# Chunk 0's layer norm: rows centred first, then transposed by products with diagonal matrices of 1/std

## The chip, the cores and the metric

The kernel runs on one NeuronCore of a Trainium2 chip. A core has five engines with queues of their own: TensorE (PE; its weight loads are shown apart as PEld), VectorE (DVE), ScalarE (ACT), GpSimd (POOL) and SyncE (SP, which here issues the transfers). The metric is the device time of one execution in microseconds; lower is better.

## What is computed

The input x has 2048 rows of 512 bf16 values. A first layer norm is followed by a spectral filter (a real two-dimensional Fourier transform, a product with complex weights, and the inverse transform), added to x. The sum h goes through a second layer norm and a two-layer network with a squared ReLU, added to h:

```python
x = A_x
h = x + irfft2(rfft2(_layernorm(x)) * (A_w_r + 1j * A_w_i))
u = _layernorm(h)                      # (h - m) / sqrt(v + 1e-5), over 512 columns
r = relu(einsum("bsd,df->bsf", u, B_w1) + B_b1)      # 512 -> 1792
out = h + einsum("bsf,fd->bsd", r * r, B_w2) + B_b2  # 1792 -> 512
```

The layer norms have no weights of their own.

## The kernel before

The 2048 rows are 16 groups g of 128 rows. The transforms are products with cosine and sine tables that are made on the chip. After the inverse transform along the rows lies its intermediate result T2 in SBUF; from there on everything is done group by group, and the groups are taken together in five chunks for the network: (0,1), (2,3,4), (5..8), (9..12), (13..15) (`CHUNKS`, L696). Two matrix products with W1 and W2 per chunk make up most of the remaining work.

The stretch between the last transform step and the first product with W1 is called the drain here. In it chunk 0 is on its own way:

- `d5` (L709, tasks pd-g-e): two products for each of the two column parities e of group g, into a PSUM bank. `deo` (L716, tasks EO-g-e) copies each result, 128x256, to SBUF.
- `d6` (L799, tasks py-g-0, py-g-1, py-g-2): four products that add up in one bank (tag `sg`, two banks, one for each group): x itself through the identity matrix (k=0), the even columns (k=1), the odd columns (k=2, two products). The bank py-g then holds h for group g.
- Statistics. The mean of h is known beforehand (nm1 is its negative). For group 0 ScalarE squares h minus the mean with a sum as a second output (task ss-0, L814, profile line L674); for group 1 VectorE uses the batch-norm statistics (tasks st2 and ss-1, L817 and L819). ScalarE takes the root (sd-0-g, L820), VectorE the reciprocal (r2-0-g, L823) and the product nr2 = nm1 * rs2 (L825).
- `un0` (L828): the normalised rows u, 128x512 bf16; ScalarE for group 0 (L833), VectorE for group 1 (L831).
- `tr0` (L839): four 128x128 transposes of each group on TensorE, into a bank of tag `po` (two banks), with bf16 results.
- `et0` (L846): one copy of 128x512 for each group to UT, the operand of the first products with W1. ScalarE or VectorE, whichever the planner finds ready.
- `hb` (L836): h + b2, from the bank py-g, on VectorE, after UT is complete. With its end the `sg` bank is free.

The first two blocks f of the product with W1 (`up`, L904) are split by group for chunk 0: the half of group 0 is task pf-f, the half of group 1 is task ph-0-f. pf-0 writes a bank of tag `ph`, pf-1 one of tag `po`; later blocks use `ph` and the two `sg` banks in turn.

Chunk 1's groups 2, 3 and 4 already begin in the drain: four products (`s5`, L736, tasks p5-g, tag `pp` with three banks), a copy of half of them on ScalarE (`od`, L745), two sums on VectorE (`lv1`, L750, tasks q-g-0 and q-g-1), and nine small products (`s6`, L759, tasks p6-g) into another `pp` bank.

The order of the instructions is set by a planner, `Plan` (L34 to L137). Each task has an engine (or a choice of two), a cost, what it reads, and a priority. `run` (L89) takes, again and again, over all engines, the task with the earliest planned start `r`; if two engines have the same start, VectorE goes first (L118). A result that passes from one engine to another costs `HOP` (L39: PE 0.20, ACT 0.17, DVE 0.15), on the same engine 0.1 for VectorE and ScalarE. The tasks are emitted in the order in which they are picked, and `pin` (L22) keeps each engine in that order. The planner knows how many banks a tag has and gives the one that comes free first (`slot`, L77). The framework adds the waits between engines.

`bank` (L687) hands out the PSUM banks. If the planner expects TensorE to stand idle for over 0.4 us before the task, it puts products of a zero matrix into the new bank first (L689, L690), one for each 0.0625 us of 0.6 of the gap, at most 20. They are called fillers below.

Of the kernel before, what the change touches and what calls it, by code (L numbers as in the profile page):

```python
# [9 lines left out]
ALU = mybir.AluOpType  # L10
ACT = mybir.ActivationFunctionType
# [22 lines left out]
class Plan:  # L34
# [13 lines left out]
    def add(self, eng, w, fn, reads=(), writes=(), prio=0.0, alloc=None, at=0.0, shared=False, lag=0.0,  # L48
            uses=(), order=()):
        many = isinstance(eng, tuple)  # L50
        ways = dict(zip(eng, w)) if many else {eng: w}
        t = dict(many=many, eng=None, ways=ways, w=0.0, fn=fn, reads=list(reads), writes=list(writes), prio=prio, alloc=alloc, at=at,
                 shared=shared, lag=lag, end=None, order=list(order), n=len(self.tasks))
        self.tasks.append(t)
        for k in t["writes"]:
            self.made.setdefault(k, []).append(t)
        for k in set(t["reads"]) | set(t["writes"]) | set(uses):
            self.use.setdefault(k, []).append(t)
# [29 lines left out]

    def run(self):  # L89
        left = {}  # L90
# [6 lines left out]
        while any(left.values()):  # L97
            best = None
            for e, ts in left.items():
                cand = []  # L100
                for t in ts:
                    r = self.ready(t, e)
                    if r is None:
                        continue
                    if t["alloc"]:
                        s, _ = self.slot(t["alloc"][0])
                        if s is None:
                            continue
                        r = max(r, s)
                    r = max(r, self.free[e])  # L110
                    cand.append((r, t))
                    if r <= self.free[e] + 1e-9:
                        break
# [11 lines left out]
            if t["alloc"]:  # L125
                tag, key = t["alloc"]
                _, old = self.slot(tag)
                if old is not None:
                    self.held[tag].remove(old)
                self.held[tag].append(key)  # L130
            self.gap = r - self.free[e]
            t["end"] = r + t["w"]
            self.free[e] = t["end"]
            for k in t["ways"]:
                left[k].remove(t)
            self.log.append((r, t["end"], e, t["writes"]))
            t["fn"](*([e] if t["many"] else []))  # L137
# [3 lines left out]
def kernel(  # L141
# [47 lines left out]
    st2 = persist.tile([P, 6], FP32, name="st2")  # L189
    EO = persist.tile([P, 2, 2, 256], BF16, name="EO")  # L190
    junk = persist.tile([P, D], BF16, name="junk")
    fz = persist.tile([P, 512], BF16, name="fz")
# [295 lines left out]
    for pr, first in ((0, 1), (1, 1), *((p, 0) for p in range(8))):  # L488
# [45 lines left out]
        if pr == 0 and first:  # L534
# [11 lines left out]
            for u in range(2):  # L546
# [3 lines left out]
                    order=[("X", 0, 0)] * u, writes=[("X", 0), ("Xu", u)] + [("X", 0, 0)] * (1 - u),  # L550
                    alloc=None if u else ("AB", ("X", 0)))
        elif pr > 0 and not first:
# [29 lines left out]
            def ea(pr=pr, ab=ab):  # L582
                t = buf(fwd, ab, "AB", [P, 2, 2, 256], BF16, 3)
                sc.copy(t[:].rearrange("p u r c -> p (u r c)"), T["p3", pr][:])  # L584
            act(0.93, ea, z + 1, reads=[("p3", pr)], writes=[ab], alloc=("AB", ab))
            if ab[0] == "AB":
# [6 lines left out]
                for h in range(2):  # L593
                    dve(0.34, lambda pr=pr, h=h: bf(pr, h), z, reads=[("AB", pr)],
                        order=[("Xh", pr)] * h,
                        writes=[("X", pr)] + [("Xh", pr)] * (1 - h), alloc=("X", ("X", pr)) if h == 0 else None)

# [8 lines left out]
        for u in range(2) if pr == 0 else ():  # L606
            dve(0.61, lambda u=u, prod=prod: prod(0, u, 1), z, reads=[("Xu", u), ("Wn", 0), ("Wn", 1)], uses=[("X", 0)],
                order=["mh"] * u, writes=[("m", 0)] + ["mh"] * (1 - u), alloc=None if u else ("m", ("m", 0)))
        if pr:
# [6 lines left out]
        for r in range(2):  # L616
            dve(0.34, lambda pr=pr, r=r: zz(pr, r), z, reads=[("m", pr)],
                order=[("Zh", pr)] * r,
                writes=[("Z", pr)] + [("Zh", pr)] * (1 - r), alloc=("Z", ("Z", pr)) if r == 0 else None)
        if pr > 0:  # L620
# [8 lines left out]
            for h in range(2):  # L629
                dve(0.34, lambda pr=pr, h=h: fold(pr, h), z, reads=[("Z", pr)],  # L630
                        order=[("Mh", pr)] * h,
                    writes=[("M", pr)] + [("Mh", pr)] * (1 - h), alloc=("M", ("M", pr)) if h == 0 else None)

# [29 lines left out]
        if pr < 7:  # L663
            act(0.97, et, z + 3, reads=[("p4", pr)], writes=["T2", "T2a"])
        else:
            for h in range(2):
                eng = ("ACT", "DVE")[h]
                add(eng, (0.24, 0.22)[h], lambda et=et, h=h, eng=eng: et(COPY[eng], 7, 0, 2, 2 * h, 2 * h + 2), prio=z,
                    reads=[("p4", 7, h)], writes=["T2a"])
                add(eng, (0.52, 0.6)[h], lambda et=et, h=h, eng=eng: et(COPY[eng], 7, 2, G, 2 * h, 2 * h + 2), prio=z + 90,  # L670
                    reads=[("p4", 7, h)], order=["T2a"], writes=["T2"])

# [56 lines left out]
    for c, (a, b) in enumerate(CHUNKS):  # L729
# [3 lines left out]
        for g in range(a, b):  # L733
            z = late + g
            if c > 0:
# [18 lines left out]
                for i in range(2):  # L754
                    dve(0.36, lambda g=g, i=i: lv1(g, i), z, reads=[("p5", g), ("od", g)],
                        order=[("qh", g)] * i + [("un", 1)] * (c == 1),
                        writes=[("q", g), ("qh", g)] if i == 0 else [("q", g)], alloc=("qb" if g in BY_PE2 else "q", ("q", g)) if i == 0 else None)

# [15 lines left out]
                else:  # L774
# [11 lines left out]
                    for k in range(4):  # L786
                        dve(0.25, lambda g=g, k=k: lv2(g, k), z, reads=[("q", g)], order=[("Rh", g)], writes=[("R", g)])

# [8 lines left out]
        if c == 0:  # L797
            for g in range(2):
# [9 lines left out]
                for k in range(3):  # L808
                    add("PE", 0.22, lambda g=g, k=k, d6=d6: d6(g, k),
                        reads=[["ident"], [("EO", g, 1), ("EI", 3)], [("EO", g, 0)]][k],  # L810
                        order=[("pd", 1, 0) if k == 0 else ("pd", g, 0)] + [("py", g, j) for j in range(k)], uses=[("py", g)],
                        writes=[("py", g, k)], prio=-5000.0 + g - 50 * (k == 0), alloc=("sg", ("py", g)) if k == 0 else None)
                if g == 0:
                    act(0.9, lambda: sq_of(T["py", 0][:], 0), -30.0, reads=[("py", 0, 2), "nm1", "sqrt"], writes=[("ss", 0)],  # L814
                        uses=[("py", 0)])
                else:
# [7 lines left out]
                    writes=[("r2", 0, g)])  # L824
                dve(0.16, lambda g=g: ve.tensor_tensor(nr2[:, g:g + 1], nm1[:, g:g + 1], rs2[:, g:g + 1], ALU.mult), -30.0,  # L825
                    reads=[("r2", 0, g), "nm1"], writes=[("n2", 0, g)])

                def un0(g=g):  # L828
                    u = buf(ffn, ("u", 0), "u2", [P, 4, D], BF16, 2) if g == 0 else T["u", 0]
                    if g:  # L830
                        ve.tensor_scalar(u[:, 1, :], T["py", 1][:], nm1[:, 1:2], rs2[:, 1:2], ALU.add, ALU.mult)  # L831
                    else:
                        sc.activation(u[:, 0, :], T["py", 0][:], ACT.Identity, scale=rs2[:, 0:1], bias=nr2[:, 0:1])  # L833
                add(("ACT", "DVE")[g], (0.6, 0.7)[g], un0, reads=[("r2", 0, g), ("n2", 0, g)], writes=[("un", g)] + ["una0"] * (1 - g),
                    order=["una0"] * g, uses=[("py", g), ("u", 0)], prio=-30.0, alloc=None if g else ("u2", ("u", 0)))
                dve(0.69, lambda g=g: ve.tensor_tensor(hb[:, g, :], T["py", g][:], b2b[:], ALU.add), -10.0,  # L836
                    reads=[("un", g), ("FW", 3)], order=[("UT", 0)] * OWN, writes=[("hb", g)], uses=[("py", g)])

                def tr0(g=g):  # L839
                    p = bank(("pt", 0, g), "po", 2, BF16)  # L840
                    for d in range(ND):
                        pe.transpose(p[:, P * d:P * d + P], T["u", 0][:, g, bass.ts(d, P)], ident[:])
                add("PE", 0.24, tr0, reads=[("un", g)], writes=[("pt", 0, g)], uses=[("u", 0)], prio=early + 3,
                    alloc=("po", ("pt", 0, g)))

                def et0(e, g=g):  # L846
                    u = buf(ffn, ("UT", 0), "UT", [P, 4, ND, P], BF16, 2) if g == 0 else T["UT", 0]
                    COPY[e](flat(u[:, g]), T["pt", 0, g][:, 0:D])
                add(("ACT", "DVE"), (0.57, 0.43), et0, reads=[("pt", 0, g)], order=["UT0a"] * g,
                    writes=[("UT", 0), "UT0b" if g else "UT0a"], prio=-30.0, alloc=None if g else ("UT", ("UT", 0)))  # L850
        else:
# [8 lines left out]
            for g in range(a, b):  # L860
                def un(e, g=g, a=a, c=c):
# [8 lines left out]
                    order=[("una", a)] * (g > a), uses=[("u", c)],  # L870
                    writes=[("un", g)] + [("una", a)] * (g == a), prio=z, shared=True, alloc=("u2", ("u", c)) if g == a else None)
            for g in range(a, b):
# [3 lines left out]
                def turn(c=c, i=g - a):  # L876
                    u = buf(ffn, ("UT", c), "UT", [P, 4, ND, P], BF16, 2) if i == 0 else T["UT", c]
                    sy.dma_start(u[:, i], T["u", c][:, i, :], transpose=True)
                add("SP", 1.2, turn, reads=[("un", g)], order=[("UTh", c)] * (g > a), uses=[("u", c)], lag=2.8,
                    writes=[("UT", c)] + [("UTh", c)] * (g == a), prio=z, alloc=("UT", ("UT", c)) if g == a else None)  # L880
            for g in range(a, b):
# [9 lines left out]
                def et2(e, c=c, g=g, i=g - a):  # L891
                    u = buf(ffn, ("UT", c), "UT", [P, 4, ND, P], BF16, 2) if i == 0 else T["UT", c]
                    COPY[e](flat(u[:, i]), T["pt", g][:, 0:D])
                add(("ACT", "DVE"), (0.57, 0.43), et2, reads=[("pt", g)], order=[("UTh", c)] * (g > a),
                    writes=[("UT", c)] + [("UTh", c)] * (g == a), prio=z, alloc=("UT", ("UT", c)) if g == a else None)

        for f in range(NF):
# [24 lines left out]
            def sqr(c=c, f=f, n=n):  # L922
# [3 lines left out]
            dve(0.07 + 0.07 * n, sqr, z, reads=[("rl", c, f)], order=[("act", c, 0)] * (f > 0),  # L926
                writes=[("act", c, f), ("act", c)], alloc=("act", ("act", c)) if f == 0 else None)
        for i in range(n):
            g = a + i
            for h in range(2) if g == G - 1 else (None,):  # L930
# [12 lines left out]
                def out_(g=g, h=h, cs=cs):  # L943
# [5 lines left out]
                    writes=[("out", g)], uses=[("ot", g)], prio=nxt())  # L949
    plan.run()  # L950
    pin(tc, nc)
# [29 lines left out]
```

## Time and profile before

| | |
|---|---|
| time, median of 3 runs | 161.3 us (160.69 to 161.52) |
| profiled execution: span from first to last instruction | 159.2 us |
| profiled execution: its own time | not given apart from the runs; the median lies 2.1 us above the span |
| PE / PEld busy | 96% / 58% of the span |
| DVE / ACT / POOL busy | 76% / 64% / 21% |
| granted TensorE clock | 1.000 |
| drain, from the first pd product to the first product with W1 | 46.47 to 51.89 us |

Busy shares are shares of the span. A row of the timeline gives the start, the duration (from start to the acknowledged end), the engine, the line, the operation, and the output and input tiles; tile names are those of the program (sg is the bank of py-g, rs the array rs2, UT the transposed rows). Rows in succession on one line are merged ("x2"). A row of the chain gives start, duration, engine and line, and only what lies on the chain that ended last. A window row gives the stretch, its length, then the busy time and number of instructions of each engine, the granted clock and the share of the DMA engines.

### The profile page before, as it was taken

How to read it: one execution, taken by the hardware profiler on the slowest of the kernel's cores; microseconds unless marked ns; L12 is line 12 of the kernel's file. 1: busy time of each engine (PE TensorE's matmuls, PEld its weight loads, DVE VectorE, ACT ScalarE, POOL GpSimd, SP SyncE). 2: the span in 40 equal slices, each digit the busy share in tenths (PEclk: the TensorE clock that was granted, in tenths of full speed). 3: DMA queues.
4: the chain of work that ended last, by engine and by line, in shares of the span. 5: the costliest groups of instructions: out<-in, count | busy, mean ns of one | idle time of the engine just before them, and what ended most of it. 6: DMA issues, size and time to landing. Idle time of an engine off the chain costs nothing.

```text
span 159.2 us, 2899 instructions
## 1 busy us (share of the span) xinstructions
PE 152.4 (96%) x1026; PEld 92.2 (58%) x1035; DVE 120.6 (76%) x325; ACT 102.2 (64%) x187; POOL 32.9 (21%) x83
## 2 busy tenths in 40 slices
PE   6999999999988999999999999999999999999992
PEld 4587876777666876565644544444544444565471
DVE  6999999999967996889863898992599962285221
ACT  8989689998976897297900889530488820188100
POOL 8798700000000024022230004440002240000000
PEclk9999999999999999999999999999999999999999
DMA  5958999992000001102332000224100212010011
GB/s 137 326 185 236 210 272 223 399 353 77 0 4 0 0 4 35 35 33 33 37 64 68 33 0 4 57 44 132 33 2 4 55 43 66 33 35 4 0 66 33
DMA packets 21018, 13.43 MB, mean 84 GB/s; under 512 B 9739, under 2 KB 19723, under 8 KB 21003
## 3 DMA queue, kind: packets, MB, share of 16 engines
q1 hardware_dynamic: 21002, 13.25, 30.7%
q8 instruction: 8, 0.13, 0.4%
q14 instruction: 8, 0.06, 0.1%
HBM read 8.92 MB, written 3.01 MB: 75 GB/s over the span
## 4 chain that ended last, share of the span: by engine, by line
PE 70%; DVE 18%; DMA 4%; issue 3%; SPq 1%; ACT 0%; POOL 0%; DVEq 0%
PE po L936 30%; PE sg L907 20%; PE ph L907 10%; DVE m L605 5%; DMA xs<-in_A_x_dram 4%; DVE Z L615 4%; DVE st L387 3%; DVE M L626 2%; DVE M L628 2%; DVE X L591 2%; PE pp L762 1%; PE pp L769 1%; SPq L266 1%; PE s_p L507 1%; PE s_p L652 1%
## 5 line engine op out<-in xcount | busy, mean ns | idle before, releaser
L936 PE MATMUL po<-W,act 128*128 128x512 bf16 (+1 forms) x229 | 48.7, 366 | 0.5
L919 ACT ACTIVATE rl<-sg,b1f 128x384 bf16<-128x384 f32 (+2 forms) x46 | 27.3, 602 | 21.8 <-PE sg L907 20.6
L907 PEld LDWEIGHTS <-W 128*128 128x128 bf16 x288 | 26.8, 98 | 19.6 <-issue 0.2
L907 PE MATMUL sg<-UT,W 128*128 128x384 bf16 (+2 forms) x184 | 37.2, 337 | 0.0
L936 PEld LDWEIGHTS <-act 128*128 128x128 bf16 x238 | 23.2, 98 | 24.1
L925 DVE TENSOR_TENSOR act<-rl 128x384 bf16<-128x384 bf16 (+2 forms) x70 | 25.0, 366 | 6.5 <-ACT rl L919 6.0
L945 DVE TENSOR_TENSOR ot<-po,hb 128x512 bf16<-128x512 f32 (+1 forms) x17 | 11.2, 659 | 21.0 <-PE po L936 20.7
L854 POOL TENSOR_SCALAR rs<-ss 128x1 f32<-128x1 f32 x14 | 5.5, 394 | 91.5 <-ACT junk L674 91.5
L919 ACT ACTIVATE rl<-ph,b1f 128x512 bf16<-128x512 f32 (+2 forms) x23 | 13.9, 602 | 10.0 <-PE ph L907 9.4
L907 PE MATMUL ph<-UT,W 128*128 128x512 bf16 (+3 forms) x96 | 19.9, 330 | 0.1
L790 DVE TENSOR_TENSOR hs<-pp,xs 128x512 bf16<-128x512 f32 x14 | 9.7, 690 | 2.3 <-PE pp L762 1.3
L674 ACT ACTIVATE junk<-hs,nm 128x512 bf16<-128x512 bf16 x14 | 10.0, 713 | 0.1
L486 PE MATMUL m_p<-U,EF 128*128 128x512 bf16 (+1 forms) x46 | 9.5, 337 | 0.0
L387 DVE BATCH_NORM_STATS2 st<-xs 128x6 f32<-128x512 bf16 x14 | 9.0, 673 | 0.6 <-DMA xs<-in_A_x_dram 0.6
L785 DVE TENSOR_TENSOR R<-q 128x127 bf16<-128x127 f32 x40 | 9.4, 283 | 0.0
L794 DVE TENSOR_TENSOR hb<-hs,b2b 128x512 f32<-128x512 bf16 x14 | 9.2, 683 | 0.0
L237 PEld LDWEIGHTS <-fz 128*128 128x128 bf16 x80 | 6.4, 110 | 4.6 <-issue 2.6
L856 POOL TENSOR_TENSOR rs<-rs,mhalf 128x1 f32<-128x1 f32 x14 | 8.3, 594 | 1.2
L584 ACT CAST AB<-m_p 128x1024 bf16<-128x1024 f32 x7 | 7.1, 1019 | 1.2 <-PE m_p L486 1.1
L752 DVE TENSOR_TENSOR q<-pp,od 128x256 f32<-128x256 f32 x20 | 7.6, 414 | 0.0
L507 PEld LDWEIGHTS <-Bt 128*128 128x128 bf16 x64 | 6.2, 98 | 1.5 <-DVE Bt L442 0.2
L652 PEld LDWEIGHTS <-M 128*128 128x128 bf16 x56 | 5.2, 98 | 3.1 <-DVE M L626 1.4
(160 smaller groups left out, 229.5 us busy)
## 6 DMA issues: line engine op xcount, KB each, us to landing
W<-in_B_w_dram SPq DMA_DIRECT2D x2, 1792.0 KB, 10.5
out_dram<-ot SPq DMA_DIRECT2D x15, 128.0 KB, 1.8
xs<-in_A_x_dram SPq DMA_DIRECT2D x4, 256.0 KB, 3.8
xs<-in_A_x_dram SPq DMA_DIRECT2D x2, 512.0 KB, 6.8
W<-wx SPq DMA_DIRECT2D x2, 448.0 KB
W<-in_A_w_r_dram SPq DMA_DIRECT2D x1, 512.0 KB, 8.2
W<-in_A_w_i_dram SPq DMA_DIRECT2D x1, 512.0 KB, 6.2
wx<-in_A_w_r_dram SPq DMA_DIRECT2D x1, 448.0 KB
```

The lines of the kernel that those rows point to most:

```text
L387: ve.bn_stats(st[:], xs[:, g, :])
L486: mm(o.rearrange("p (j i e) -> p j i e", e=2, i=RUN), lhsT=w, rhs=U[:, q, s].rearrange("p (j e i) -> p j i e", e=2, i=RUN), **k)
L674: sc.activation(junk[:], src, ACT.Square, bias=nm1[:, g:g + 1], accum_out=ss2[:, g:g + 1])
L785: ve.tensor_tensor(o, x, y, (ALU.add, ALU.subtract, ALU.subtract, ALU.add)[k])
L790: dve(0.66, lambda g=g: ve.tensor_tensor(hs[:, g, :], T["p6", g][:], xs[:, g, :], ALU.add), z, reads=[("p6", g)], writes=[("hs", g)])
L794: add(("DVE", "POOL")[HBP], (0.62, 1.3)[HBP], lambda g=g: (ve, gp)[HBP].tensor_tensor(hb[:, g, :], hs[:, g, :], b2b[:], ALU.add), prio=lat ...
L856: pool(0.57, lambda p0=p0, p1=p1: gp.tensor_tensor(rs2[:, p0:p1], rs2[:, p0:p1], mhalf[:, 0:p1 - p0], ALU.pow), z, reads=[("sd", c, k)], w ...
L907: mm(p[:, P * i0:P * i1], lhsT=W1[:, d, bass.ts(f, P)], rhs=T["UT", c][:, i0:i1, d, :], start=(d == 0), stop=(d == ND - 1))
L919: sc.activation(r[:, 0:P * n], T["ph", c, f][:, 0:P * n], ACT.Relu, bias=b1f[:, f:f + 1], scale=1.0)
L925: ve.tensor_tensor(t[:, f, 0:P * n], r[:, 0:P * n], r[:, 0:P * n], ALU.mult)
L936: mm(p[:, cs], lhsT=T["act", c][:, f, bass.ts(i, P)], rhs=W2[:, f, cs], start=(f == 0), stop=(f == NF - 1))
L945: ve.tensor_tensor(o[:, cs], T["po", g, h][:, cs], hb[:, g, cs], ALU.add)
```

## The change

Chunk 0's group g is now only centred from its bank (task cen-g): u = h minus the mean, on VectorE for group 0 and on ScalarE for group 1. This needs no standard deviation. 1/std comes in with the transpose: VectorE makes a 128x128 diagonal matrix of it in bf16 (dg-g-0, the identity times rs2), and another of what bf16 has lost of it (dl-g). TensorE multiplies each block of u with the first (task pt-0-g-0) and then with the second (pt-0-g-1) in the same bank, now fp32. The product nr2 is not made for chunk 0. The copies to UT are halved (UTa-g-h, 128x256), and may be on either engine.

Tasks get names, and `run` takes an order written by hand for each engine, `DRAIN`; as long as an engine has entries left, only the task of that name can be picked for it. The start times are still planned, and `bank` still adds its fillers.

```diff
-    def run(self):
+    def run(self, line=None):
+        lines = {e: v.split() for e, v in (line or {}).items()}
...
-                for t in ts:
+                for t in ts if not lines.get(e) else [t for t in ts if t["name"] == lines[e][0]]:
...
+            if lines.get(e):
+                lines[e].pop(0)
...
+    dg = persist.tile([P, 2, 2, P], BF16, name="dg")
...
-                dve(0.16, lambda g=g: ve.tensor_tensor(nr2[:, g:g + 1], nm1[:, g:g + 1], rs2[:, g:g + 1], ALU.mult), -30.0,
-                    reads=[("r2", 0, g), "nm1"], writes=[("n2", 0, g)])
-
-                def un0(g=g):
+                def cen(g=g):
                     u = buf(ffn, ("u", 0), "u2", [P, 4, D], BF16, 2) if g == 0 else T["u", 0]
                     if g:
-                        ve.tensor_scalar(u[:, 1, :], T["py", 1][:], nm1[:, 1:2], rs2[:, 1:2], ALU.add, ALU.mult)
+                        sc.activation(u[:, 1, :], T["py", 1][:], ACT.Identity, bias=nm1[:, 1:2])
                     else:
-                        sc.activation(u[:, 0, :], T["py", 0][:], ACT.Identity, scale=rs2[:, 0:1], bias=nr2[:, 0:1])
-                add(("ACT", "DVE")[g], (0.6, 0.7)[g], un0, reads=[("r2", 0, g), ("n2", 0, g)], writes=[("un", g)] + ["una0"] * (1 - g),
-                    order=["una0"] * g, uses=[("py", g), ("u", 0)], prio=-30.0, alloc=None if g else ("u2", ("u", 0)))
+                        ve.tensor_scalar(u[:, 0, :], T["py", 0][:], nm1[:, 0:1], None, ALU.add)
+                add(("DVE", "ACT")[g], 0.63, cen, reads=[("py", g, 2), "nm1"], writes=[("cen", g)], uses=[("py", g), ("u", 0)],
+                    order=[("cen", 0)] * g, prio=-30.0, alloc=None if g else ("u2", ("u", 0)))
+                dve(0.12, lambda g=g: ve.tensor_scalar(dg[:, g, 0], ident[:], rs2[:, g:g + 1], None, ALU.mult), -30.0,
+                    reads=[("r2", 0, g), "ident"], writes=[("dg", g, 0)])
+                dve(0.2, lambda g=g: ve.scalar_tensor_tensor(dg[:, g, 1], ident[:], rs2[:, g:g + 1], dg[:, g, 0], ALU.mult,
+                                                             ALU.subtract), -30.0,
+                    reads=[("dg", g, 0)], writes=[("dg", g, 1), ("un", g)] + ["una0"] * (1 - g), name=f"dl-{g}")
...
-                def tr0(g=g):
-                    p = bank(("pt", 0, g), "po", 2, BF16)
+                def tr0(g=g, k=0):
+                    p = bank(("pt", 0, g), "po", 2) if k == 0 else T["pt", 0, g]
                     for d in range(ND):
-                        pe.transpose(p[:, P * d:P * d + P], T["u", 0][:, g, bass.ts(d, P)], ident[:])
-                add("PE", 0.24, tr0, reads=[("un", g)], writes=[("pt", 0, g)], uses=[("u", 0)], prio=early + 3,
-                    alloc=("po", ("pt", 0, g)))
-
-                def et0(e, g=g):
-                    u = buf(ffn, ("UT", 0), "UT", [P, 4, ND, P], BF16, 2) if g == 0 else T["UT", 0]
-                    COPY[e](flat(u[:, g]), T["pt", 0, g][:, 0:D])
-                add(("ACT", "DVE"), (0.57, 0.43), et0, reads=[("pt", 0, g)], order=["UT0a"] * g,
-                    writes=[("UT", 0), "UT0b" if g else "UT0a"], prio=-30.0, alloc=None if g else ("UT", ("UT", 0)))
+                        mm(p[:, P * d:P * d + P], lhsT=T["u", 0][:, g, bass.ts(d, P)], rhs=dg[:, g, k],
+                           start=k == 0 and d == 0, stop=k == 1 and d == ND - 1)
+                for k in range(2):
+                    add("PE", 0.24, lambda g=g, k=k, tr0=tr0: tr0(g, k), reads=[("cen", g), ("dg", g, k)],
+                        order=[("pt", 0, g, 0)] * k, writes=[("pt", 0, g), ("pt", 0, g, k)], uses=[("u", 0)], prio=early + 3,
+                        alloc=None if k else ("po", ("pt", 0, g)))
+
+                def et0(e, g=g, h=0):
+                    u = buf(ffn, ("UT", 0), "UT", [P, 4, ND, P], BF16, 2) if (g, h) == (0, 0) else T["UT", 0]
+                    COPY[e](flat(u[:, g, 2 * h:2 * h + 2]), T["pt", 0, g][:, 256 * h:256 * h + 256])
+                for h in range(2):
+                    add(("ACT", "DVE"), (0.37, 0.36), lambda e, h=h, et0=et0: et0(e, h=h), reads=[("pt", 0, g)],
+                        order=["UTa"] * (g + h > 0), writes=[("UT", 0), "UT0b" if g else "UT0a"] + ["UTa"] * (g + h == 0),
+                        prio=-30.0, alloc=None if g + h else ("UT", ("UT", 0)), name=f"UTa-{g}-{h}")
...
-    plan.run()
+    DRAIN = {
+        "PE": "pd-0-1 pd-0-0 pd-1-1 pd-1-0 py-0-0 py-0-1 py-0-2 py-1-0 py-1-1 py-1-2 p5-2 p5-4 p5-3 "
+             "pt-0-0-0 pt-0-0-1 pt-0-1-0 pt-0-1-1 pf-1 pf-0 p6-3 ph-0-0",
+        "ACT": "EO-0-0 EO-1-1 EO-1-0 ss-0 sd-0-0 cen-1 sd-0-1 od-4 od-3 UTa-0-0 UTa-0-1 UTa-1-1 UTa-1-0 "
+              "od-2",
+        "DVE": "EO-0-1 cen-0 st2 r2-0-0 ss-1 dg-0-0 dl-0 r2-0-1 dg-1-0 dl-1 q-3-0 q-3-1 hb-0",
+    }
+    plan.run(DRAIN)
     pin(tc, nc)
```

In the order before, py-1-0 came between py-0-0 and py-0-1, group 2 was the first of chunk 1, and its p6-2 came after the first blocks of the product with W1; each of ScalarE and VectorE had two of the four EO copies, and one of the two copies to UT. By the list, all four halves of UT's copies are on ScalarE, as VectorE's list names none of them until hb-0, which waits for them.

## Prediction

> **What bounds the kernel now.** I read the clock first (mean granted clock 1.000, so no throttling to explain), then the chain of waits that ended last. Its summary and its stretch around the change:
>
> ```profile
> PE 70%; DVE 18%; DMA 4%; issue 3%; SPq 1%; ACT 0%; POOL 0%; DVEq 0%
> ...
> 48.95 0.71 DVE st L817
> 49.69 0.18 DVE mv L819
> ...
> 49.95 0.17 DVE nr L825
> 50.14 0.79 ACT u L833
> 50.98 0.41 PE po L842 x4
> 51.41 0.44 DVE UT L848
> 51.89 0.38 PE ph L907 x4
> 52.27 0.22 PE po L907 x4
> 52.50 0.34 PE ph L907 x4
> 52.83 0.22 PE po L907 x4
> 53.05 0.96 PE sg L907 x8
> ```
>
> From 51.89 to 156.16 us the chain is TensorE work almost without a gap: the rest of the kernel is TensorE-bound, and any shift of the point from which TensorE is full goes one to one into the end, as long as nothing starves it later. Ahead of that point it waits for chunk 0's layer norm. Next I cut this stretch into windows (columns PE, PEld, DVE, ACT, POOL):
>
> ```profile
> 49.43:50.98 1.55, 1.12 (x21) 0.94 (x18) 1.33 (x7) 1.33 (x4) 0.00 (x0) 1.00 0.00 0
> 50.98:51.89 0.91, 0.79 (x8) 0.50 (x9) 0.82 (x3) 0.56 (x3) 0.00 (x0) 1.00 0.00 0
> 52.89:53.85 0.96, 0.96 (x12) 0.78 (x9) 0.96 (x4) 0.96 (x3) 0.00 (x0) 1.00 0.00 0
> ```
>
> The 1.12 us of PE in the first is filler (17 products with zeros, L690). Useful work is missing for 1.55 us there; for 0.17 between the two transposes (51.20 to 51.37), 0.28 before L907 starts (51.61 to 51.89) and 0.12 before its second half (52.33 to 52.45); in the third window eight products of 0.109 (0.87) take 0.96, because the second `sg` bank is freed by hb-1. Together 2.2 us: the most that this change could win, 1.4%. The timeline of ScalarE and VectorE gives the durations:
>
> ```profile
> 48.58 0.69 ACT L674 ACTIVATE junk<-sg,nm 128x512 bf16<-128x512 f32 x1 [0.77 <-PE sg L807]
> 49.39 0.29 ACT L820 ACTIVATE rs<-ss,eps 128x1 f32<-128x1 f32 x1
> 50.14 0.78 ACT L833 ACTIVATE u<-sg,nr,rs 128x512 bf16<-128x512 f32 x1
> 50.82 0.64 ACT L747 COPY od<-pp 128x256 f32<-128x256 f32 x2
> 51.81 0.59 ACT L848 COPY UT<-po 128x512 bf16<-128x512 bf16 x1 [0.35 <-PE po L842]
> ...
> 50.51 0.81 DVE L831 TENSOR_SCALAR u<-sg,nm,rs 128x512 bf16<-128x512 f32 x1
> ```
>
> A start comes ahead of the previous row's end: two od copies of 0.366 take 0.64, a pitch of 0.28; after L833 the pitch is 0.68, after L820 0.24.
>
> **The Trainium skill.** (1) "PSUM — Partial Sum Buffer", section "PSUM bank collisions raise a hardware error": two engines may not touch one bank at once, "ACT↔DVE too", reads against reads, and the back end adds a dependency between two such instructions. The trace of before can't confirm it: no bank there is read by both engines without a data dependency. In the new order both py banks are. (2) "Perfetto Trace Analysis", "Optimizing Scalar/DVE Operations": a profiled latency is about twice the engine's overhead, the second half overlapping the next instruction; the pitches above agree. (3) "VectorE: DVE Perf Modes", "The perf-mode tier table": any PSUM operand caps the mode, fp32 at 1x; the 512-wide VectorE rows from PSUM (678 to 698 ns) agree.
>
> **The change, part by part.** All times on the trace's clock.
>
> *Order of the products.* py-1-0 (0.215, an L802 row) goes behind py-0-2, so py-0's last product starts at 47.99 instead of 48.21; py-1's stays at 48.64. EO-0-1 moves to VectorE, the other three to ScalarE at a pitch of 0.28 (47.22, 47.51, 47.80, done 48.17): all are there before their products. VectorE starts 0.31 after a last product's start (48.64 to 48.95): cen-0 can start at 48.30. Gain so far 0.22.
>
> *Centring.* cen-0 has no row. A cast of this shape takes 0.690; the two-scalar form 0.810, so one scalar about 0.75 (bounds 0.68 and 0.81). It ends at 49.05. cen-0 and ss-0 both wait for py-0-2 alone. In the planner they get the same start, and its tie rule emits VectorE first. By (1) ss-0, on ScalarE, must then wait for cen-0. I take this: ss-0 at 49.09, not 48.36. Behind it on ScalarE stand sd-0-0, cen-1, sd-0-1, two od and four UTa; TensorE waits for the last of these. Without that wait the 0.73 is gone. st2 (48.97) is not delayed; it ends before cen-1, so py-1's bank costs nothing.
>
> *ScalarE's queue from there*: ss-0 0.77 with its accumulator read, to 49.86; sd-0-0 at 49.90, pitch 0.24; cen-1 at 50.14, as L833, pitch 0.68; sd-0-1 at 50.82, pitch 0.24; od-4 and od-3 at 0.28 each; UTa-0-0 at 51.62, UTa-0-1 at 51.90 (as EO, 0.373), done 52.27. It is without a gap: ScalarE is the bound of the stage.
>
> *Diagonals on VectorE*: nr (0.159, twice) goes. A one-scalar bf16 row of 256 (KR, L403) takes 0.282, a 1-wide row 0.15: I take 0.25 for dg. Three-operand rows take 0.251 at 32 wide and 0.469 at 256: 0.34 for dl at 128. r2-0-0 waits for sd-0-0 (50.23) with ss-1 behind it (done 50.50, before 50.82, so free); dg-0-0 at 50.41, dl-0 at 50.70, done 51.04. r2-0-1 51.15, dg-1-0 51.34, dl-1 51.63, done 51.97. At the lower ends row 0 is no faster, since ScalarE reaches UTa-0-0 only at 51.62; at +0.1 each UTa-0-0 slips by under 0.1.
>
> *Products.* Sixteen of 0.055 for eight: 0.44 more of TensorE, in a gap where it has nothing else (49.83 to 52.3); free, and 0.44 if that gap closes. Row 1's last starts at 52.19, so UTa-1-1 is at 52.44 and UTa-1-0 done at 53.09.
>
> *Filler.* `bank` adds products when the planned gap exceeds 0.4. By the planner's costs before, the gap ahead of pt is 1.79: 17 fillers, which the trace shows. For after I get 0.79 (7 fillers, harmless) and, ahead of pf-1, 4x0.37+0.17 minus 1.24 = 0.41: 3 fillers. They write into pf-1's `po` bank, which pt-0-0 holds until UTa-0-1 has read it: 3x0.056 = 0.17 **on** the path.
>
> *Refilling TensorE.* pf-1 52.32+0.17 = 52.49, pf-0 52.71, p6-3 52.93 (0.44; q-3-1 on VectorE behind dl-1, done 52.65), ph-0-0 at 53.37 (UTa-1-0 is there). Work done by then: 0.22+0.22+0.44 = 0.88; before, the same 0.88 was done at 52.89. **Loss 0.48.** hb-0 now stands behind q-3 (52.6 to 53.3) and hb-1 follows (to 53.9); the `sg` banks are wanted at 53.8 and 54.25, so the 0.09 stall goes. Sum +0.39. Nothing is moved on POOL or SP.
>
> *Later.* Element 3 is now ahead of 2 in chunk 1. The last UT copy of chunk 1 lands at 65.42 and its first product is at 66.96: 1.5 us of cover; beyond it the cost is one to one.
>
> Against the profiled span: 159.2+0.4 = 159.6; the runs' median lies 2.1 above the span, so **161.7**.
>
> **Rivals.**
> *Readers overlap.* If no wait is added on the py banks, ScalarE starts ss-0 at 48.36 and cen-1 at 49.41; UTa-0-1 is done at 51.55, pf-1 at 51.77, ph-0-0 at 52.64: 0.25 gained, with the stall 0.34: 161.0; without fillers 160.8. For it: two addresses only read need no data dependency. Against: the page in (1). 0.20, shortened chains of other kinds included.
> *p6-3's bank.* `pp` has three banks, held by p5-2, p5-4, p5-3. The planner gives p6-3 the one freed first (p5-3). If it gets the oldest, p5-2's, TensorE waits for q-2, which stands on VectorE behind hb-0 and hb-1 and needs od-2, behind the UTa: done 54.5, p6-3 at 54.6 instead of 52.93, ph-0-0 behind it: +1.65 more, 163.4. It decides slower by itself once that wait exceeds 0.4. For: banks so far came free in order, so before shows neither. Against: the planner would count a bank that it doesn't get. 0.10.
> *Chunk 1 late.* The reordered elements use up the 1.5 us and over 0.4 more: 162.2 to 163. 0.10.
>
> **From cases to numbers.** Forecast 0.60 (own range 160.9 to 162.3: durations 0.2, fillers 0.17, ordering afterwards 0.4). Within 0.5%, about 0.8 us, is what a measurement can tell from no change. Faster: 0.03 of the forecast and 0.09 of the overlap; slower: 0.08 of the forecast, 0.10 and 0.10 of the two others; same the remaining 0.60. The range reaches into overlap and late chunk: 160.6 to 162.7.
>
> **What would show it.** Right: L674's row on `sg` starts only after the VectorE row cen-0 has ended, near 49.1; ScalarE gapless from there to 52.3; seven and three fillers; pf-1 near 52.5 with p6 right behind pf-0. Wrong: ss-0 and cen-0 starting together; a PE wait at p6-3; a TensorE gap near 67.

## The result, and the profile after

| | before | after |
|---|---|---|
| time, median of 20 runs each | 161.24 us (160.69 to 161.87) | 161.65 us (161.15 to 162.44) |
| after / before | | 1.0028, 95% interval 1.0014 to 1.0041 |
| span of the profiled execution | 159.2 us | 159.5 us |
| first pd product (start) | 46.47 us | 46.36 us |
| last output row (start) | 156.16 us | 156.50 us |
| between the two | 109.69 us | 110.14 us |

The change costs 0.45 us: by the medians' ratio (0.0028 of 161.24) and by the last row of the table. That row is the better measure in a trace. The place of the first pd product lies between 46.2 and 47.3 us from one execution to the next, because of work ahead of the drain, which no kernel here changes; from that product on the executions can be laid over each other. Below, "total" means this distance; 0.11 is to be taken off the prediction's times when they are compared with the trace of after.

The chain of waits of after, between the last products of group 0 and the network's first `sg` blocks (start, duration, engine, line):

```profile
47.94 0.11 PE sg L811
48.05 0.12 PE sg L812
48.17 0.02 issue
48.19 0.76 DVE u L835
...
49.04 0.79 ACT junk L679 x2
49.83 0.02 issue
49.85 0.30 ACT rs L825
50.15 0.02 issue
50.17 0.16 DVE rs L828
50.34 0.09 DVE mv L824
50.43 0.02 issue
50.45 0.27 DVE dg L838
50.71 0.04 issue
50.76 0.38 PE po L849 x4
...
52.28 0.31 PE po L695 x3
52.59 0.22 PE po L922 x4
...
53.95 0.87 PE sg L922 x8
```

TensorE's rows start up to 0.17 us later in a chain than in a timeline (pf-1 above at 52.59, in the timeline at 52.43); distances are taken within one view.

Before, this chain went through group 1's statistics on VectorE. Now it starts with cen-0 (L835), and behind it stands ss-0 (L679), which doesn't use what cen-0 makes. The timeline of ScalarE says the same, in the bracket, which gives the idle time before a row and what ended it:

```profile
49.04 0.69 ACT L679 ACTIVATE junk<-sg,nm 128x512 bf16<-128x512 f32 x1 [1.01 <-DVE u L835]
...
49.85 0.29 ACT L825 ACTIVATE rs<-ss,eps 128x1 f32<-128x1 f32 x1
50.05 0.67 ACT L833 ACTIVATE u<-sg,nm 128x512 bf16<-128x512 f32 x1
50.62 0.28 ACT L825 ACTIVATE rs<-mv,eps 128x1 f32<-128x1 f32 x1
50.80 0.63 ACT L752 COPY od<-pp 128x256 f32<-128x256 f32 x2
51.56 1.40 ACT L858 CAST UT<-po 128x256 bf16<-128x256 f32 x4
```

The inputs of L679 are `sg` and `nm`; its releaser is the row that writes `u`. What the two have in common is the bank py-0 and the mean (`nm`), and both only read them; an experiment below shows that `nm` isn't needed for such a wait. The timelines of VectorE and of TensorE of after:

```profile
48.19 0.75 DVE L835 TENSOR_SCALAR u<-sg,nm 128x512 bf16<-128x512 f32 x1 [0.82 <-PE sg L812]
...
50.17 0.16 DVE L828 RECIPROCAL rs<-rs 128x1 f32<-128x1 f32 x1 [0.62 <-ACT rs L825]
...
50.45 0.26 DVE L838 TENSOR_SCALAR dg<-ident,rs 128x128 bf16<-128x128 bf16 x1
50.74 0.35 DVE L840 SCALAR_TENSOR_TENSOR dg<-ident,rs,dg 128x128 bf16<-128x128 bf16 x1
```

```profile
49.32 0.56 PE L695 MATMUL po<-fz 128*128 128x128 bf16 x7
50.76 1.52 PE L849 MATMUL po<-dg,u 128*128 128x128 bf16 x16 [0.88 <-DVE dg L838]
52.26 0.33 PE L695 MATMUL po<-fz 128*128 128x128 bf16 x3
52.43 0.39 PE L922 MATMUL po<-UT,W 128*128 128x128 bf16 x4
52.65 0.39 PE L922 MATMUL ph<-UT,W 128*128 128x128 bf16 x4
52.87 0.61 PE L774 MATMUL pp<-qb,KI 128*128 128x127 bf16 x8
...
53.79 1.04 PE L922 MATMUL sg<-UT,W 128*128 128x256 bf16 x8
54.66 0.60 PE L922 MATMUL ph<-UT,W 128*128 128x256 bf16 x4
```

Seven fillers fall into idle time ahead of the diagonal products; three stand directly ahead of pf-1 (52.26 to 52.43). The eight `sg` products take 54.66 - 53.79 = 0.87 us where they took 0.96: the stall on the second `sg` bank is gone. From the first of them to the last output row it is 102.71 us. Before, from its own 52.89 and without one block of nine p6 products (0.45; before, all three of chunk 1 lie behind that point, after, only two) and without the stall (0.09), it was 103.27 - 0.54 = 102.73. So everything that was lost was lost ahead of 53.79.

### The profile page after: what moved, and what is told of

It is laid out like the page before. It is cut to its first block, busy times and chain, and to the rows that moved or that the text cites. A ratio compares the mean times of both kernels' runs of the same rounds, so it can differ in the third digit from the quotient of the medians.

```text
span 159.5 us, 2915 instructions
## 1 busy us (share of the span) xinstructions
PE 152.2 (95%) x1036; PEld 92.0 (58%) x1036; DVE 120.0 (75%) x324; ACT 103.0 (65%) x192; POOL 32.6 (20%) x83
## 4 chain that ended last, share of the span: by engine, by line
PE 73%; DVE 16%; POOL 5%; issue 3%; ACT 1%; DVEq 0%; POOLq 0%; ACTq 0%
PE po L951 30%; PE sg L922 20%; PE ph L922 10%; DVE m L610 5%; DVE Z L620 4%; DVE M L631 2%; DVE M L633 2%; DVE X L596 2%; DVE st L392 2%; POOL KR L408 1%; PE pp L767 1%; POOL rs L399 1%; PE pp L774 1%; PE po L849 1%; PE s_p L415 1%
## 5 line engine op out<-in xcount | busy, mean ns | idle before, releaser
L951 PE MATMUL po<-W,act 128*128 128x512 bf16 (+1 forms) x238 | 50.0, 367 | 0.0
L679 ACT ACTIVATE junk<-hs,nm 128x512 bf16<-128x512 bf16 x14 | 10.0, 713 | 0.2
```

The costliest lines, as they stand in the source:

```text
L679: sc.activation(junk[:], src, ACT.Square, bias=nm1[:, g:g + 1], accum_out=ss2[:, g:g + 1])
L951: mm(p[:, cs], lhsT=T["act", c][:, f, bass.ts(i, P)], rhs=W2[:, f, cs], start=(f == 0), stop=(f == NF - 1))
```

## Experiments

Theory A is the prediction's: cen-0 on VectorE and ss-0 on ScalarE read one PSUM bank, the one is made to wait for the other, and this wait is the loss. Against it stand the work that the change adds (diagonals, sixteen products for eight, fillers) and the written order. Line numbers are those of after. All totals, beside the ratios of the timed runs to the kernel before (a total is that of one execution; it agrees with the timed ratio within 0.3 us, so smaller differences are read from rows of the traces):

| kernel | edit to after | total, us | against before | ratio (95%) |
|---|---|---|---|---|
| after | | 110.14 | +0.45 | 1.0028 (1.0014 to 1.0041) |
| e1_cen0_act | cen-0 on ScalarE | 110.04 | +0.35 | 1.0029 (1.0018 to 1.0040) |
| e1_cen0_twice | cen-0 done twice | 110.95 | +1.26 | 1.0095 (1.0064 to 1.0127) |
| e1_ss0_first | ss-0 ahead of cen-0 | 110.35 | +0.66 | 1.0046 (1.0033 to 1.0058) |
| e1_nofill | no fillers ahead of pf-1 | 109.97 | +0.28 | 1.0026 (1.0013 to 1.0039) |
| e2_cen0_act_same | cen-0 on ScalarE, fillers as in after | 109.70 | +0.01 | 0.9994 (0.9982 to 1.0007) |
| e2_cen0_act_order | the same, other order, none ahead of pf-1 | 109.49 | -0.20 | 0.9981 (0.9968 to 0.9994) |
| e2_list_only | old norm, written order | 109.66 | -0.03 | 0.9992 (0.9979 to 1.0005) |
| e2_no_list | new norm, planner's order | 111.06 | +1.37 | 1.0080 (1.0058 to 1.0102) |
| e3_order_only | e2_cen0_act_order with cen-0 on VectorE | 110.19 | +0.50 | 1.0028 (1.0017 to 1.0039) |
| e3_no_remainder | without dl | 109.92 | +0.23 | 1.0020 (1.0009 to 1.0030) |
| e3_cen0_act_order_again | e2_cen0_act_order repeated | 109.49 | -0.20 | 0.9986 (0.9976 to 0.9997) |
| e4_no_later_fill | e2_cen0_act_order, no later fillers | 109.26 | -0.43 | 0.9963 (0.9952 to 0.9974) |

**cen-0 twice.**

```diff
-                        ve.tensor_scalar(u[:, 0, :], T["py", 0][:], nm1[:, 0:1], None, ALU.add)
+                        for _ in range(2):
+                            ve.tensor_scalar(u[:, 0, :], T["py", 0][:], nm1[:, 0:1], None, ALU.add)
```

> The new kernel with cen-0 executed twice in succession on VectorE. Theory A: ss-0 starts one pitch later (0.68), and all of it is on the path: 0.65 us slower than the new kernel, 162.3, ratio 1.007. Theory B: ss-0 starts as before; VectorE's st2 is 0.68 later, but ss-1 is not wanted until cen-1 is done; within 0.2 us of the new kernel.

The timeline of ScalarE:

```profile
49.69 0.69 ACT L679 ACTIVATE junk<-sg,nm 128x512 bf16<-128x512 f32 x1 [1.82 <-DVE u L836]
```

ss-0's wait grows from 1.01 to 1.82 us, and the total by 0.81. The loss follows the length of cen-0 nearly one to one. (The ratio's +0.67% is 1.1 us; its interval is wide, but excludes that nothing happened.)

**ss-0 first.** The two readers are swapped, with nothing else changed.

```diff
-                    order=[("cen", 0)] * g, ...
+                    order=[("cen", 0)] if g else [("ss", 0)], ...
```

> The new kernel with ss-0 emitted ahead of cen-0, the order on each engine unchanged. Theory A: the wait turns round. ss-0 starts 0.75 us earlier, cen-0 only when ss-0's square has ended, with st2 behind it, and cen-1 waits for st2: 0.3 us slower than the new kernel (0.2 to 0.5), 161.95, ratio 1.0045. Theory B: neither row moves, and the time stays.

ScalarE and then VectorE of this kernel:

```profile
48.38 0.69 ACT L679 ACTIVATE junk<-sg,nm 128x512 bf16<-128x512 f32 x1 [0.22 <-PE sg L812]
...
50.58 0.69 ACT L833 ACTIVATE u<-sg,nm 128x512 bf16<-128x512 f32 x1 [1.10 <-DVE st L822]
```

```profile
49.19 0.75 DVE L835 TENSOR_SCALAR u<-sg,nm 128x512 bf16<-128x512 f32 x1 [1.69 <-ACT junk L679]
49.86 0.69 DVE L822 BATCH_NORM_STATS2 st<-sg 128x6 f32<-128x512 f32 x1
```

The wait turns round: now cen-0 waits for ss-0. So it isn't a property of one engine or of one instruction. A second pair shows up too: cen-1 (ScalarE) waits for st2 (VectorE), and these two have only the bank py-1 in common: the only input of st2 is `sg`, so that a shared `nm` can't be the reason. Behind the late cen-0, st2 is late as well, so this order is worse than after's, 1.0046.

**cen-0 on ScalarE, first try.** If one engine has both readers of py-0, neither waits for another engine.

```diff
-                        ve.tensor_scalar(u[:, 0, :], T["py", 0][:], nm1[:, 0:1], None, ALU.add)
+                        sc.activation(u[:, 0, :], T["py", 0][:], ACT.Identity, bias=nm1[:, 0:1])
...
-        "ACT": "... ss-0 sd-0-0 cen-1 sd-0-1 od-4 ...
+        "ACT": "... ss-0 sd-0-0 cen-0 sd-0-1 cen-1 od-4 ...
...
-        "DVE": "EO-0-1 cen-0 st2 ...
+        "DVE": "EO-0-1 st2 ...
```

The fillers ahead of a group's diagonal products were held to seven.

> The new kernel with cen-0 moved from VectorE to ScalarE, behind sd-0-0; cen-1 goes behind sd-0-1; the fillers ahead of pt are kept at seven. No bank is then read by two engines at once. Theory A (ss-0 waits because VectorE reads its bank): ss-0 starts 0.35 us after py-0's last product, 0.75 earlier than in the new kernel; though ScalarE has 0.58 more to do, the whole is 0.5 us faster than the new kernel (0.4 to 0.6), 161.15, a ratio to before of 0.9995. Theory B (ss-0 is late for another reason, such as its place behind the EO copies, and the loss comes from the copies to UT and the order): ss-0 stays where it is, and cen-0 comes on top: 0.4 to 0.6 slower than the new kernel, ratio 1.006.

The time missed it, 1.0029, though ss-0 did start early: 48.62 - 46.73 = 1.89 us behind the first pd product, in after 49.04 - 46.36 = 2.68. TensorE's timeline shows why:

```profile
51.00 0.39 PE L695 MATMUL po<-fz 128*128 128x128 bf16 x4
...
52.19 0.66 PE L695 MATMUL po<-fz 128*128 128x128 bf16 x9 [0.28 <-ACT UT L858]
52.69 0.39 PE L922 MATMUL po<-UT,W 128*128 128x128 bf16 x4
```

With new planned times `bank` put four fillers between the two groups and nine ahead of pf-1: 52.19 to 52.69, 0.50 us on the path where after has 0.17. As a test of what the wait costs this run is inconclusive; it had to be repeated with the fillers held.

**cen-0 on ScalarE, fillers as in after** (seven, none, three):

```diff
-        for _ in range(min(20, int(plan.gap * 0.6 / 0.0625)) if plan.gap > 0.4 else 0):
+        for _ in range((({0: 7, 1: 0}[key[2]] if key[:2] == ("pt", 0) else 3 if key == ("ph", 0, 1) else min(20, int(plan.gap * 0.6 / 0.0625))) if plan.gap > 0.4 else 0)):
```

> As the earlier kernel with cen-0 on ScalarE behind sd-0-0 and cen-1 behind sd-0-1, but with the fillers exactly as in the new kernel: seven ahead of pt, none between the two pt groups, three ahead of pf-1 (the earlier one had four and nine, and the nine took 0.50 us). Theory A (the wait of ss-0 for VectorE's reader of the same bank costs the time): 0.4 us faster than the new kernel (0.3 to 0.55), 161.25, ratio to before 1.0000. Theory B (the copies and the order cost it, and the seat of cen-0 does not matter): as the new kernel, ratio 1.0028, or slower by ScalarE's further 0.58.

```profile
48.76 0.69 ACT L679 ACTIVATE junk<-sg,nm 128x512 bf16<-128x512 f32 x1 [0.22 <-PE sg L812]
...
49.77 0.67 ACT L835 ACTIVATE u<-sg,nm 128x512 bf16<-128x512 f32 x1
50.34 0.28 ACT L825 ACTIVATE rs<-mv,eps 128x1 f32<-128x1 f32 x1
50.53 0.68 ACT L833 ACTIVATE u<-sg,nm 128x512 bf16<-128x512 f32 x1
...
51.61 1.22 ACT L858 CAST UT<-po 128x256 bf16<-128x256 f32 x4
```

This timeline of ScalarE is to be set beside after's. From the first pd product, ss-0 starts at 48.76 - 46.88 = 1.88 us where it was 49.04 - 46.36 = 2.68: 0.80 earlier. The first copy to UT starts at 4.73 where it was 5.20: 0.47 earlier. The rest is eaten by cen-0 in ScalarE's own queue (50.34 - 49.77 = 0.57), less a gap of about 0.23 ahead of the first copy that after has and this kernel hasn't. The total falls by 0.44, and the ratio to 0.9994. This one move gives back all of the loss, with the added work still there. That VectorE has one row less isn't the reason: in after it stood idle for 0.62 us ahead of the first reciprocal (50.17), until ScalarE's root was there.

**No fillers ahead of pf-1.**

```diff
+        ... if plan.gap > 0.4 and key != ("ph", 0, 1) else 0
```

> The new kernel without the three fillers ahead of pf-1. If they wait for UTa-0-1 and lie on the path (theory A's account of the sum), pf-1 starts 0.17 us earlier and the whole is 0.17 faster than the new kernel: 161.48, ratio 1.0015. If TensorE would have stood idle anyway, no change.

The total falls by 0.17, which is the three fillers' own time; the timed ratio, 1.0026, doesn't resolve it.

**No remainder.** This kernel leaves out dl-0 and dl-1 and the eight products with them, so that 1/std is taken in bf16 alone; seven and three fillers.

> The new kernel without the second diagonal: dl-0, dl-1 and the eight products with them are left out, so 1/std is taken in bf16 only; the fillers are kept at seven and three. By the chain of waits of the new kernel dl-0 lies on the path: UTa-0-0 starts when ScalarE comes to it, after od-3, 0.15 to 0.2 earlier, and the copies then run without a gap: 0.2 us faster than the new kernel (0.1 to 0.3), ratio to before 1.0015. If the remainder were the main cost of the change, 0.5 or more faster than the new kernel, below 0.9995.

```profile
51.87 1.21 ACT L855 CAST UT<-po 128x256 bf16<-128x256 f32 x4
```

The first copy to UT starts 51.87 - 46.91 = 4.96 us behind the first pd product (in after 5.20), and the total is 0.22 less than after's, ratio 1.0020. By the trace the remainder is on the path, with about half of the loss; the ratio's interval overlaps after's and doesn't show it by itself.

**The list alone, and none.** e2_list_only has the old layer norm of chunk 0 under a written order (groups' transposes, then pf-1; od-4 and od-3 ahead of the copy to UT on ScalarE). e2_no_list has the new one and `plan.run()` for `plan.run(DRAIN)`.

> The written order alone: the old normalisation (nr2, then one row on ScalarE and one on VectorE with mean and 1/std), the old eight transposes with bf16 results, the old two copies (group 0 on VectorE, group 1 on ScalarE), but py-0 ahead of py-1, the EO copies as in the new kernel, and chunk 1's group 3 first with p6-3 ahead of the second half. No bank is read by two engines at once. From the rows of before: py-0 is 0.2 earlier and p6-3 fills the wait for the second half: 0.1 us faster than before (0.3 faster to 0.1 slower), ratio 0.9994. If the written order itself were what costs the time, 0.3 to 0.5 slower than before.

> The centring and the diagonal products alone, in the order that the planner finds by itself: py-1-0 between py-0-0 and py-0-1, cen-1 ahead of sd-0-0 on ScalarE, group 2 first, two halves of UT on each engine, 14 fillers ahead of pt and none later. Theory A: ss-0 again starts only when cen-0 has ended, now 0.2 later, and cen-1 adds 0.58 ahead of the root: 0.8 us slower than before (0.5 to 1.1), ratio 1.005. Theory B (the list costs the time): as before or faster.

The list by itself changes nothing that can be measured (0.9992). Without it the new layer norm is much worse than with it, 1.0080, by more than expected. Rows of its VectorE and ScalarE timelines:

```profile
48.51 0.75 DVE L835 TENSOR_SCALAR u<-sg,nm 128x512 bf16<-128x512 f32 x1 [0.44 <-PE sg L812]
```

```profile
49.35 0.69 ACT L679 ACTIVATE junk<-sg,nm 128x512 bf16<-128x512 f32 x1 [1.56 <-DVE u L835]
...
50.03 0.68 ACT L833 ACTIVATE u<-sg,nm 128x512 bf16<-128x512 f32 x1
50.60 0.29 ACT L825 ACTIVATE rs<-ss,eps 128x1 f32<-128x1 f32 x1
```

The same wait again: ss-0 starts 49.35 - 48.51 = 0.84 us behind cen-0, in after 49.04 - 48.19 = 0.85. Then cen-1 is taken ahead of sd-0-0, so that the root, and the diagonals with it, come 0.57 us later still. Behind the diagonals the chain runs over the copies to UT, which are on both engines here, and over hb-0, which frees the bank of the first `sg` block:

```profile
53.61 0.69 DVE hb L843
...
54.34 0.60 PE sg L922 x4
```

The planner also put four fillers ahead of pf-0 (52.66), where none were expected; they aren't on this chain.

**Other order, fewer fillers.** e2_cen0_act_order has cen-0 on ScalarE, none of the fillers ahead of pf-1, p5-3 ahead of p5-4, and od-4 behind the first two copies to UT:

```diff
-        "ACT": "... cen-1 sd-0-1 od-4 od-3 UTa-0-0 UTa-0-1 UTa-1-1 UTa-1-0 "
+        "ACT": "... cen-0 sd-0-1 cen-1 od-3 UTa-0-0 UTa-0-1 od-4 UTa-1-1 UTa-1-0 "
```

e3_order_only has these edits with cen-0 left on VectorE, and e3_cen0_act_order_again repeats the former beside it.

> Both centrings on ScalarE as in the kernel beside it, no fillers ahead of pf-1, p5-3 ahead of p5-4 on TensorE, and ScalarE's order od-3, UTa-0-0, UTa-0-1, od-4, UTa-1-1, UTa-1-0, so that the first copies go out as soon as pt-0-0-1 is there. Theory A: TensorE starts pf-1 5.25 us after the first pd product instead of 6.07, and by the end of the second sg block it is 0.4 us ahead of the kernel before (0.2 to 0.5): 160.85, ratio 0.9975. Theory B: no faster than before.

> The kernel that was fastest so far, with cen-0 back on VectorE (and so cen-1 back ahead of sd-0-1): only ScalarE's order od-3, UTa-0-0, UTa-0-1, od-4, UTa-1-1, UTa-1-0, p5-3 ahead of p5-4, and no fillers ahead of pf-1. Theory A (the two readers of py-0 cost the time): pt-0-0-1 is no earlier than in the new kernel, so the order gains nothing and the fillers' 0.17 is all: 161.45, ratio to before 1.0017 (1.0005 to 1.0025). Theory C (in that kernel it was the order of ScalarE that gained): 0.998 as there.

> The fastest kernel so far once more, to compare it with its neighbours on one chip: 0.4 us faster than before by the stretch of the drain, 0.3 by the times so far: ratio 0.998 (0.997 to 0.999).

With cen-0 on ScalarE 0.9981 and 0.9986, with cen-0 on VectorE 1.0028. So order and fillers aren't what gives the gain: 110.19 - 109.49 = 0.70 us hang on the engine of cen-0 (and on cen-1's place in ScalarE's queue, which goes with it). e3_order_only was expected at 1.0017 and is no better than after: the 0.17 of fillers saved is offset by four that the planner puts in later, at 86.98 us (4 x 0.055 = 0.22). In all three kernels of this order the rest, from the first `sg` block to the last output row, takes 102.93 or 102.94 us instead of 102.71.

**Without the later fillers.** e2_cen0_act_order with fillers only ahead of the pd products (five) and of pt-0-0 (seven).

```diff
+        for _ in range(({0: 7, 1: 0}[key[2]] if key[:2] == ("pt", 0) else 5 if key[0] == "pd" else 0) if plan.gap > 0.4 else 0):
```

> The fastest kernel so far without four fillers that the planner had put in near 86 us of its trace, at the start of a chunk, where TensorE was never idle (its order made the planner see a gap there). By the windows they take 4x0.056 = 0.22 us on the path: 0.22 faster than that kernel, ratio to before 0.9970 (0.9960 to 0.9980). If TensorE had to wait there anyway, the ratio stays at 0.998 to 0.9985.

```profile
49.80 0.56 PE L695 MATMUL po<-fz 128*128 128x128 bf16 x7
50.50 1.52 PE L849 MATMUL po<-dg,u 128*128 128x128 bf16 x16
52.03 0.38 PE L922 MATMUL po<-UT,W 128*128 128x128 bf16 x4
...
53.40 1.04 PE L922 MATMUL sg<-UT,W 128*128 128x256 bf16 x8
```

TensorE's timeline has pf-1 directly behind the diagonal products (52.03; 5.18 us from the first pd product at 46.85, in after 52.43 - 46.36 = 6.07), and the rest takes 102.71 again. Ratio 0.9963: of all versions here the fastest, ahead of the kernel before by 0.6 us in the timed runs and by 0.43 in the trace.

## Why the prediction was right

The forecast was 161.7 us by one mechanism, +0.39 on the trace; measured are 161.65 and +0.45. Step by step, the prediction's times less 0.11:

- **The wait of ss-0 for cen-0** (ss-0 at 48.98): 49.04, with the releaser named in the trace. It was taken from the Trainium skill, "PSUM — Partial Sum Buffer", section "PSUM bank collisions raise a hardware error", which has the back end add a dependency even between two reads. The trace of before couldn't show it; the runs do, in both directions: 1.01 and 1.82 us of idle time ahead of ss-0, against 0.22 where no row of VectorE is ahead of it on its bank, and 1.69 ahead of cen-0, against 0.82 in after. What puts the wait in, the framework or a later stage of the build, no run shows. The rival that readers overlap is refuted by it, and with cen-0 on ScalarE the 0.44 comes back.
- **cen-0's price** (0.75, by the row between a cast and the two-scalar form): 0.75. dg 0.25 and dl 0.34: 0.26 and 0.35.
- **cen-1** (pitch 0.68, as L833 before): 50.62 - 50.05 = 0.57, and 0.67 long for 0.78. This term was mis-sized, by 0.11. The row that was taken has two per-row operands, scale and bias; cen-1 has a bias alone. The trace of before held a row of that kind: L674 starts at 48.58, and the row behind it on ScalarE at 49.16, 0.58 later.
- **"ScalarE is the bound of the stage", without a gap to 52.27:** wrong. After od-3 ScalarE could have begun the first copy near 51.33 (50.80 and two pitches of about 0.27); it begins at 51.56, as the second half of the products of group 0 starts at 51.14, when dl-0 is done. VectorE's dg and dl and the products bind there, and e3_no_remainder shows their worth, 0.22. That the time came out is partly luck: cen-1 was 0.11 quicker and the two roots together 0.10 (pitches of 0.20 and 0.18 for 0.24), and this gap took it up (first copy predicted at 51.51, found at 51.56).
- **"Sixteen of 0.055 for eight ... free":** in TensorE's own time, yes (the last starts near 52.1, and the fillers behind it only at 52.26); in the path they aren't, for the reason just given.
- **Fillers**, seven and three, 0.17 on the path: exactly so, and e1_nofill gives 0.17 back in its total.
- **Refilling**: pf-1 predicted at 52.38, found at 52.43; p6-3 directly behind pf-0, so the rival of a wait at p6-3's bank is refuted; the `sg` stall is gone as forecast. *Chunk 1 late* is refuted by the unchanged 102.71. (Its cover of 1.5 us set a landing against a row of the chain; in the timeline of before that product starts at 66.79, so that the cover was 1.4.)

Of the possible gain of 2.2 us nothing arrived. The earlier py-0 (0.22) was more than used up by a wait of about 0.8 that no data asks for; the longer way over two diagonals (0.22) and the fillers (0.17) came on top. This isn't the whole account: e4_no_later_fill, with neither that wait nor those fillers, gains 0.43 by the trace, and between its p5 products and pf-1 still lie 52.03 - 49.80 = 2.23 us without work on the network (before, up to pf-0, 51.89 - 49.43 = 2.46). How much of that can be won is not shown.

## What to carry to other kernels

Before an operand in PSUM is given to a second engine, list everyone who reads that bank. Here two readers on two engines ran one after the other, in both orders, and ss-0, as the second, was late by 0.80 us, the duration of the first (0.75) and a little more. Giving both to one engine won 0.44 us back, though that engine's queue got longer. Merely letting the other reader go first did not help (1.0046), as more work waited behind the one that was then late. The planner here knows only data dependencies, and by its costs both had the same start. And after any change of order, look where the fillers have landed: here up to 0.3 us of them moved onto the path and hid the effect that was to be measured.

## What was not expected of the hardware

- An ACTIVATE of 128x512 from PSUM takes 0.67 us with a bias for each row, where 0.78 had been taken from a row with scale and bias (L833 of after and of before). The VectorE forms of this shape: 0.69 (batch-norm statistics), 0.75 with one scalar for each row, 0.81 with two.
- A filler costs its full 0.055 us where the product behind it could otherwise have started: 0.17 for three (after), 0.22 for four (e3_order_only), 0.50 for nine (e1_cen0_act).
